# A scheduled attention and feed-forward kernel: the flag branch ahead of a split last output, GpSimd's normalisation as subtract and multiply, and a scheduler that knows the time of queued transposes

## The chip, the cores and the metric

One Trainium2 chip, one of its cores. The metric is the device time of one execution in microseconds (us). In the profile PE is TensorE (matmul), PEld its weight loads, DVE is VectorE, ACT ScalarE, POOL GpSimd and SP SyncE. The granted clock is the share of TensorE's full clock that the profile records; "half clock" is a stretch at 0.5. An execution more than 1.5% above the fastest of its kernel is called slow; only fast ones are compared, and of a kernel that ran once the state is unknown.

## The reference

A pre-norm transformer block: 2048 rows of 512, 32 heads of 16, a hidden width of 1792, no learned norm weights.

```python
h  = x + A(layernorm(x))          # A: qkv = x @ wqkv; softmax(q k^T / 4) v; @ wo
h2 = h + B(layernorm(h))          # B: (gelu(x @ w_gate) * (x @ w_up)) @ w_down
```

## The kernel before

Every piece of work is an `Op` with an engine and a duration. When the kernel is built, a greedy list scheduler plays these durations through and fixes the order of instructions on each engine. Streams of work have priorities with a small random addition (`random.Random(9)`), so each seed gives another order. The softmax has 2048 tiles of 128 x 512 scores; ScalarE makes the exponentials of most of them, two tiles at a time, and VectorE the rest with integer tricks, four at a time. A fast path runs first; if a check finds the data out of its range (flag not 128), an exact path runs after it. Four parts matter here.

The normalised rows that K, Q and V are projected from. Rows 0 to 1023 are done on VectorE, rows 1024 to 2047 on GpSimd, and the latter are transposed by a DMA that SyncE issues:

```python
def ln1_norm(c, t):                       # tile t = 128 rows, c = t // 4
    if c < 2:
        yield Op("dve", 0.327, ...tensor_scalar(xn, x, mean, rstd, subtract, mult))
    else:
        yield Op("pool", 0.2,  ...tensor_tensor(htmp, mean, rstd, mult))
        yield Op("pool", 0.25, ...tensor_scalar(htmp, htmp, -1.0, mult))
        yield Op("pool", 0.77, ...tensor_scalar(xn, x, rstd, htmp, mult, add))
    # then: c < 2 TensorE transposes, else dma_start_transpose (SyncE)
```

How the scheduler counts a DMA, whatever its kind:

```python
self.t[op.eng] = start + 0.5
self.pipe = max(start + 1.5, self.pipe) + op.dur / 0.32
self.done[tok] = self.pipe + 0.8
```

The last output tile: 14 matmuls of 512 columns, one VectorE addition of the residual, one DMA. And the end of each engine's program:

```python
P.run(name, h)                            # everything of the fast path
h.wait_ge(P.sems["dve"], P.flag_count)
h.reg_load(r, flag[0:1, 0:1])
with h.If_ne(r, 128):
    ...                                   # the exact path
if name == "sp":
    for k, v in P.dma_count.items(): h.wait_ge(P.sems[k], v)
```

## Time and profile before

| | before |
|---|---|
| time, three executions | 818.12 us (818.0 to 818.47) |
| the profiled execution | span 820.5, granted clock 0.992 (it took 822.24) |
| ScalarE's first exponential / last one ends | 14.38 / 791.03 |
| from there to the end | 29.5 us |
| exponentials on ScalarE, groups on VectorE | 776, 124 |

The table is read as three stretches: up to the first exponential (the head), the run of exponentials (ScalarE's bound: 742.9 us busy of 754.2 from 36.87 to 791.03), and the tail after it. The first part of the run, in which ScalarE still stands idle between groups of eight, is called the ramp. The lines themselves stand in the prediction.

### The profile page before, as it was taken

How to read it: one execution, taken by the hardware profiler on the slowest of the kernel's cores; microseconds unless marked ns; L12 is line 12 of the kernel's file. 1: busy time of each engine (PE TensorE's matmuls, PEld its weight loads, DVE VectorE, ACT ScalarE, POOL GpSimd, SP SyncE). 2: the span in 40 equal slices, each digit the busy share in tenths (PEclk: the TensorE clock that was granted, in tenths of full speed). 3: DMA queues.
4: the chain of work that ended last, by engine and by line, in shares of the span. 5: the costliest groups of instructions: out<-in, count | busy, mean ns of one | idle time of the engine just before them, and what ended most of it. 6: DMA issues, size and time to landing. Idle time of an engine off the chain costs nothing.

```text
span 820.5 us, 20261 instructions
## 1 busy us (share of the span) xinstructions
PE 780.9 (95%) x8247; PEld 278.0 (34%) x8325; DVE 759.1 (93%) x1238; ACT 766.9 (93%) x809; POOL 251.5 (31%) x305
## 2 busy tenths in 40 slices
PE   7999999999999999999989999999999999999997
PEld 3322222222222222222223333333343444444555
DVE  7669999999999999999979999999999999999974
ACT  4799999999999999999989999999999999999961
POOL 5713355423333221221333223223232231342220
PEclk9999999999999999999989999999999999999999
DMA  6200000700110000010021000001010200110000
GB/s 206 52 8 1 7 8 7 276 21 8 26 40 14 14 8 1 14 34 14 8 40 34 20 9 21 20 17 32 8 20 15 40 8 8 28 29 16 16 22 18
DMA packets 49879, 24.33 MB, mean 30 GB/s; under 512 B 39281, under 2 KB 48753, under 8 KB 49777
## 3 DMA queue, kind: packets, MB, share of 16 engines
q1 hardware_dynamic: 49776, 22.95, 10.9%
q8 instruction: 67, 1.10, 0.6%
q14 instruction: 36, 0.29, 0.1%
HBM read 11.80 MB, written 2.10 MB: 17 GB/s over the span
## 4 chain that ended last, share of the span: by engine, by line
DVE 37%; PE 35%; ACT 16%; issue 7%; DMA 3%; POOL 1%; SPq 0%; DVEq 0%; ACTq 0%; POOLq 0%
PE pbank L1329 21%; DVE dXE L1706 16%; ACT PT L1335 13%; PE pbank L1328 13%; DVE dXE L1721 6%; DVE dXE L1719 5%; DVE dXE L1726 5%; DVE GUT L1972 1%; ACT GUT L1985 1%; DMA OAT<-OA 1%; DVE OA L1810 1%; DMA wqkv_sb<-in_A_wqkv_dram 1%; PE pbank L2052 1%; POOL dXE L1723 1%; ACT L1335 1%
## 5 line engine op out<-in xcount | busy, mean ns | idle before, releaser
L1335 ACT ACTIVATE PT<-pbank 128x1024 bf16<-128x1024 f32 x776 | 722.7, 1081 | 19.2 <-PE pbank L1329 16.7
L1329 PE MATMUL pbank<-QT,KT 32*128 32x512 bf16 (+1 forms) x2304 | 347.1, 360 | 17.8 <-ACT PT L1335 8.1
L1706 DVE TENSOR_SCALAR dXE<-pbank 128x512 uint16<-128x512 f32 x496 | 325.8, 683 | 10.9 <-PE pbank L1329 9.7
L1723 POOL TENSOR_TENSOR dXE<-dXE 128x512 f16<-128x512 f16 x124 | 157.4, 1269 | 376.2 <-DVE dXE L1721 376.2
L1329 PEld LDWEIGHTS pbank<-QT,KT 32*128 32x128 bf16 x2304 | 89.3, 91 | 292.2 <-ACT PT L1335 201.2
L1329 PE MATMUL pbank<-PT,VA 128*32 128x256 bf16 (+2 forms) x2708 | 130.7, 294 | 0.1
L1721 DVE TENSOR_TENSOR dXE<-dXE 128x1536 f16<-128x1536 f16 x124 | 124.0, 1000 | 0.9
L1719 DVE TENSOR_SCALAR dXE<-dXE 128x2048 uint16<-128x2048 uint16 x124 | 92.4, 745 | 0.1
L1726 DVE TENSOR_SCALAR dXE<-dXE 128x2048 uint16<-128x2048 uint16 x124 | 88.0, 713 | 4.8 <-POOL dXE L1723 3.5
L1329 PE MATMUL pbank<-dXE,VA 128*32 128x256 f16 (+2 forms) x1752 | 77.0, 291 | 0.7 <-DVE dXE L1726 0.5
L1328 PE MATMUL pbank<-hnT_c,wg_sb 128*128 128x256 bf16 (+2 forms) x392 | 70.0, 291 | 0.0
L1329 PEld LDWEIGHTS pbank<-PT,VA 128*32 128x32 bf16 x2708 | 48.4, 96 | 61.7 <-issue 58.8
L1328 PE MATMUL pbank<-hnT_c,wu_sb 128*128 128x256 bf16 (+2 forms) x392 | 59.3, 289 | 3.6 <-DVE GUT L2000 3.4
L1328 PE MATMUL pbank<-wd_sb,GUT 128*128 128x512 bf16 x202 | 55.3, 382 | 3.2 <-issue 3.0
L2052 PE MATMUL pbank<-ones_bf,zero_bf 128*128 128x512 bf16 x163 | 55.2, 389 | 2.1 <-issue 2.1
L1832 POOL TENSOR_TENSOR Otok<-OAT,LINV 128x128 bf16<-128x128 bf16 (+2 forms) x52 | 28.6, 564 | 82.9 <-DVE LINV L1826 82.7
L1329 PEld LDWEIGHTS pbank<-dXE,VA 128*32 128x32 bf16 x1752 | 31.1, 96 | 30.9 <-issue 18.3
L2000 DVE TENSOR_TENSOR GUT<-pbank,GUT 128x512 bf16<-128x512 f32 (+1 forms) x57 | 36.8, 674 | 2.5 <-ACT GUT L1985 1.5
L1328 PE MATMUL pbank<-xnT,wqkv_sb 128*128 128x512 bf16 (+1 forms) x152 | 38.4, 349 | 0.2 <-DVE dXE L1706 0.2
L1328 PEld LDWEIGHTS pbank<-hnT_c,wu_sb 128*128 128x128 bf16 x392 | 29.5, 98 | 25.2 <-issue 10.7
L1972 DVE CAST GUT<-pbank 128x512 bf16<-128x512 f32 (+1 forms) x53 | 35.6, 674 | 1.0 <-PE pbank L1328 0.7
L1328 PEld LDWEIGHTS pbank<-hnT_c,wg_sb 128*128 128x128 bf16 x392 | 24.8, 97 | 29.0 <-issue 26.5
(80 smaller groups left out, 344.5 us busy)
## 6 DMA issues: line engine op xcount, KB each, us to landing
xres<-in_A_x_dram SPq DMA_DIRECT2D x16, 128.0 KB, 2.2
out_dram<-out_sb SPq DMA_DIRECT2D x16, 128.0 KB, 1.7
wg_sb<-in_B_w_gate_dram SPq DMA_DIRECT2D x1, 1792.0 KB, 7.0
wu_sb<-in_B_w_up_dram SPq DMA_DIRECT2D x1, 1792.0 KB, 11.0
wd_sb<-in_B_w_down_dram SPq DMA_DIRECT2D x1, 1792.0 KB, 14.8
x_sb<-in_A_x_dram SPq DMA_DIRECT2D x3, 512.0 KB, 8.5
wqkv_sb<-in_A_wqkv_dram SPq DMA_DIRECT2D x1, 896.0 KB, 7.7
x_sb<-in_A_x_dram SPq DMA_DIRECT2D x2, 256.0 KB, 3.0
```

The source lines that it names most:

```text
L1328: return lambda e: e.matmul(o, l, r, start=start, stop=stop)
L1329: return lambda e: e.matmul(o, l, r, start=start, stop=stop, tile_position=tile)
L1335: return lambda e: e.activation(out=o, in_=i, func=func, **kw)
L1706: yield Op("dve", 0.603, lambda e: e.tensor_scalar(out=dXE[G["k"] % NX][:, 0, j, :], in0=pbank[:, b, :], scalar1=XMIN + 1024.0 * CENTER, s ...
L1719: yield Op("dve", 0.07 + 0.133 * n, lambda e: e.tensor_scalar(out=W, in0=X, scalar1=0x3ff, scalar2=0xb800, op0=ALU.bitwise_and, op1=ALU.bi ...
L1721: yield Op("dve", 0.066 + 0.267 * nd, lambda e: e.tensor_tensor(out=W[:, 0:nd, :].bitcast(F16), in0=W[:, 0:nd, :].bitcast(F16), in1=X[:, 0 ...
L1723: yield Op("pool", TPOOL, lambda e, j=j: e.tensor_tensor(out=W[:, j, :].bitcast(F16), in0=W[:, j, :].bitcast(F16), in1=X[:, j, :].bitcast( ...
L1726: yield Op("dve", 0.07 + 0.133 * (h1 - h0), lambda e, h0=h0, h1=h1: e.tensor_scalar(out=X[:, h0:h1, :], in0=X[:, h0:h1, :], scalar1=0x7c00 ...
L1832: yield Op("pool" if turned else "dve", 0.15 + 0.55 / len(slots) if turned else 0.06 + 0.28 / len(slots), lambda e, o4=o4, lx=lx, o_ap=o_a ...
L1972: yield Op("dve", 0.07 + 0.001042 * n * CHUNKS[c], lambda e: e.tensor_copy(out=o_ap, in_=i_ap), reads=[("pb", b)], writes=keys, extra=dE)
L2000: yield Op("dve", 0.07 + 0.001042 * n * CHUNKS[c], lambda e: e.tensor_tensor(out=o_ap, in0=u_ap, in1=o_ap, op=ALU.mult), reads=[("pb", b)] ...
L2052: return Op("pe", TMM, lambda e: e.matmul(pbank[:, b, :], zero_bf[:], ones_bf[:], start=False, stop=False, skip_group_check=True), reads=[ ...
```

## The change

The intent, from the code: (a) take SyncE's and ScalarE's flag branch before the last output's instructions, so that its cost lies beside other work, and let ScalarE write the last output in two halves, with the residual added by TensorE through an identity matmul; (b) tell the scheduler how long queued transposes take, and try a new seed; (c) start sooner: ones of V on VectorE, the second 512 rows' norm at a higher priority, two transpose copies on ScalarE; (d) on GpSimd, one instruction subtract-then-multiply in place of three. Cut to its core:

```diff
-        self.rng = random.Random(9)
+        self.rng = random.Random(43)
@@ the scheduler's DMA
+            if op.dma[0] in TURNS:
+                self.t[op.eng] = start + 1.25
+                self.done[tok] += TURNS[op.dma[0]]
+TURNS = dict(OAT=2.0, OT=2.0, hT=2.0, xT=0.6)
-TTAB = 1.3
+TTAB = 1.45
@@ the end of each program
-            P.run(name, h)
+            cut = P.cut.get(name, len(P.eng[name].ops))
+            P.run(name, h, 0, cut)
             h.wait_ge(P.sems["dve"], P.flag_count)
             ...
+            if cut < len(P.eng[name].ops):
+                with h.Else():
+                    P.run(name, h, cut)
@@ ones_v: four GpSimd memsets become one on VectorE
@@ ln1: priorities of the second 512 rows from 9 to -4
-        if t >= 4:
+        if t >= 8:        # epsilon added on GpSimd only for rows from 1024
@@ ln1_norm
-            yield Op("pool", 0.2, ... htmp = mean * rstd)
-            yield Op("pool", 0.25, ... htmp = -htmp)
-            yield Op("pool", 0.77, ... scalar1=rstd, scalar2=htmp, op0=mult, op1=add)
+            yield Op("pool", 0.77, ... scalar1=mean, scalar2=rstd, op0=subtract, op1=mult)
@@ ln1_T
-        if t in (0, 1, 2):
+        if t in (0, 1, 2, 4, 5):      # transpose copies on ScalarE
@@ last_down: identity matmul of h, then 14 matmuls of 256 columns, twice;
@@ last_evac: ScalarE copies each half; its DMA from SyncE, then from ScalarE
(cut: sizes assumed for loads, the bank gate of the V projections, the place of one memset,
 SyncE's last waits sorted, and two more priorities)
```

More of the change, by code (lines that the diff above doesn't have):

```diff
@@ L33, in __init__ @@
         self.dma_count = {}
+        self.dma_last = {}
+        self.cut = {}
         self.n_waits = 0
@@ L100, in dma @@
         self.dma_count[semkey] += 16
+        self.dma_last[semkey] = sum(self.dma_count.values())
         tok = (semkey, self.dma_count[semkey])
@@ L148, in finish, with run @@
         self.wait(eng, [(k, v) for k, v in self.dma_count.items() if v > 0])
-    def run(self, name, h):
+    def run(self, name, h, lo=0, hi=None):
         e = self.eng[name]
-        for (fn, waits, sig, dsem) in e.ops:
+        for (fn, waits, sig, dsem) in e.ops[lo:hi]:
             for (k, v) in waits:
@@ L1192, in emit @@
                 FP.run(name, h)
+            if cut < len(P.eng[name].ops):
+                with h.Else():
+                    P.run(name, h, cut)
             if name == "sp":
-                for k, v in P.dma_count.items():
-                    h.wait_ge(P.sems[k], v)
+                for k in sorted(P.dma_count, key=lambda k: P.dma_last[k]):
+                    h.wait_ge(P.sems[k], P.dma_count[k])
         block.tensor(lambda h: emit("pe", h))
@@ L1343, in xl @@
         def xl(c):
-            return d(x_sb[:, 4 * c:4 * c + 4, :], xv[:, 4 * c:4 * c + 4, :], ("x", c), [("x", c)], 0.5)
+            return d(x_sb[:, 4 * c:4 * c + 4, :], xv[:, 4 * c:4 * c + 4, :], ("x", c), [("x", c)], 0.32)
         yield d(x_sb[:, 0:2, :], xv[:, 0:2, :], ("x", 0, 0), [("x", 0, 0)], 0.25)
@@ L1348, in loads @@
         yield w("wq0", 0, 128, 0.3)
-        yield d(x_sb[:, 4:8, :], xv[:, 4:8, :], ("x", 1), [("x", 1)], 0.9)
-        yield w("wB", 640, 1536, 0.35)
+        yield d(x_sb[:, 4:8, :], xv[:, 4:8, :], ("x", 1), [("x", 1)], 1.05)
+        yield w("wB", 640, 1536, 0.70)
         yield xl(2)
-        yield w("wA", 128, 512, 0.42)
+        yield w("wA", 128, 512, 0.25)
         yield xl(3)
-        yield d(wo_sb[:], A_wo.rearrange("(c p) j -> p c j", p=128), "wo", ["wo"], 0.5)
+        yield d(wo_sb[:], A_wo.rearrange("(c p) j -> p c j", p=128), "wo", ["wo"], 0.3)
     def xkey(c, t):
@@ L1368, in ones_v @@
     def ones_v():
-        for q in range(4):
-            yield Op("pool", 0.6, lambda e, q=q: e.memset(VA[:, 4 * q:4 * q + 4, :, 16:17], 1.0), writes=["VA_ones"], gate=lambda: C["exp"] >= 1, port=True)
-        yield Op("pool", 0.1, lambda e: e.memset(VF[:, NVA:NVA + 15], 0.0), writes=["VA_ones"])
+        yield Op("dve", 0.62, lambda e: e.memset(VA[:, :, :, 16:17], 1.0), writes=["VA_ones"])
+        yield Op("dve", 0.1, lambda e: e.memset(VF[:, NVA:NVA + 15], 0.0), writes=["VA_ones"])
     def masks():
+        yield Op("dve", 0.5, lambda e: e.memset(pbank[:, DENSE[0], :], 0.0), writes=[("pb", DENSE[0])])
         for par in range(2):
@@ L1378, in masks @@
                      reads=[("qm", par)], writes=[("qm", par)])
-        yield Op("dve", 0.5, lambda e: e.memset(pbank[:, DENSE[0], :], 0.0), writes=[("pb", DENSE[0])])
         yield Op("dve", 0.1, lambda e: e.tensor_scalar(out=probe[:, 0:1], in0=ident32[:, 0:1], scalar1=1e6, scalar2=XMIN, op0=ALU.add, op1=ALU.max), reads=["ident32"], writes=["probe"])
@@ L1406, in ln1 @@
                 yield Op("dve", 0.1, lambda e, t=t: e.bn_aggr(out=mv[:, t, :], in_=stats[:, t, :]), reads=[("stats", t)], writes=[("mv", t)])
-                if c == 0:
+                if c < 2:
                     yield Op("dve", 0.1, lambda e, t=t: e.tensor_scalar(out=rstd[:, t:t + 1], in0=mv[:, t, 1:2], scalar1=EPS, scalar2=None, op0=ALU.add), reads=[("mv", t)], writes=[("rstd0", t)])
-                sch.add(ln1_rstd(t), 2 + 7 * c if c else -7.5)
-            sch.add(ln1_norm(c, t), 2 + 7 * c if c else -7.5)
+                sch.add(ln1_rstd(t), (-4 if c == 1 else -7.5 if c == 0 else 2 + 7 * c))
+            sch.add(ln1_norm(c, t), (-4 if c == 1 else -7.5 if c == 0 else 2 + 7 * c))
     def ln1_rstd(t):
         tt_ = slice(t, t + 1)
-        if t >= 4:
+        if t >= 8:
             yield Op("pool", 0.25, lambda e: e.tensor_scalar(out=rstd[:, tt_], in0=mv[:, t, 1:2], scalar1=EPS, scalar2=None, op0=ALU.add),
@@ L1427, in ln1_norm @@
         else:
-            yield Op("pool", 0.2, lambda e: e.tensor_tensor(out=htmp[:, tt_], in0=mv[:, t, 0:1], in1=rstd[:, tt_], op=ALU.mult),
-                     reads=[("mv", t), ("rstd", t)], writes=[("nmr", t)])
-            yield Op("pool", 0.25, lambda e: e.tensor_scalar(out=htmp[:, tt_], in0=htmp[:, tt_], scalar1=-1.0, scalar2=None, op0=ALU.mult),
-                     reads=[("nmr", t)], writes=[("nmr", t)])
             yield Op("pool", 0.77,
-                     lambda e: e.tensor_scalar(out=xn_sb[:, t % 8, :], in0=x_sb[:, t, :], scalar1=rstd[:, tt_], scalar2=htmp[:, tt_], op0=ALU.mult, op1=ALU.add),
-                     reads=[xkey(c, t), ("rstd", t), ("nmr", t)], writes=[("xn", t % 8)], gate=ok)
-        sch.add(ln1_T(c, t), 2 + 7 * c if c else -8)
+                     lambda e: e.tensor_scalar(out=xn_sb[:, t % 8, :], in0=x_sb[:, t, :], scalar1=mv[:, t, 0:1], scalar2=rstd[:, tt_], op0=ALU.subtract, op1=ALU.mult),
+                     reads=[xkey(c, t), ("rstd", t), ("mv", t)], writes=[("xn", t % 8)], gate=ok)
+        sch.add(ln1_T(c, t), (-4 if c == 1 else -8 if c == 0 else 2 + 7 * c))
     def turn(o, i, key, reads, writes, **kw):
@@ L1539, in proj_v @@
             mev.prio = T0 + 2 + 1.8 * t
-            b = yield Acquire(reads=rd)
+            b = yield Acquire(reads=rd, gate=None)
             for hf in range(2):
@@ L1849, in ofin @@
         if u == NU - 1:
-            sch.add(check(), base_dl(c) + 60)
+            sch.add(check(), base_dl(c) + 20)
     def leave(c):
@@ L2003, in up_evac, with last_down, last_evac @@
         C["pieces"] += 1
+    def last_down(c, qt):
+        q0 = g_at[c] + 128 * qt
+        for hf in range(2):
+            cs = slice(256 * hf, 256 * hf + 256)
+            b = yield Acquire(reads=["wd"], gate=lambda: C.get(("gut", c), 0) >= len(packs(c)) - 1)
+            yield Op("pe", 0.11, cols=256, fns=[MM(pbank[:, b, 0:256], ident[:], h_c[c][:, qt, cs], True, False)], reads=["ident", ("h", c, qt)], writes=[("pb", b)])
+            yield Wait(lambda: C.get(("gut", c), 0) == len(packs(c)))
+            for f0 in range(0, NFC, 7):
+                fcs = range(f0, f0 + 7)
+                yield Op("pe", 7 * 0.11, cols=256 * 7, fns=[MM(pbank[:, b, 0:256], GUT[:, fc, q0:q0 + 128], wd_sb[:, fc, cs], False, fc == NFC - 1) for fc in fcs],
+                         reads=["wd"] + [("GUT", fc, q0 // 128) for fc in fcs], writes=[("pb", b)])
+            sch.add(last_evac(c, qt, hf, cs, b), -20)
+        C["down"] += 1
+        C[("down", c)] = C.get(("down", c), 0) + 1
+        C["pieces"] += 1
+    def last_evac(c, qt, hf, cs, b):
+        t = first_t[c] + qt
+        oi = t % 2
+        yield Wait(lambda: hasattr(P, "flag_count"))
+        yield Op("act", 0.28, lambda e: e.activation(out=out_sb[:, oi, cs], in_=pbank[:, b, 0:256], func=ACT.Copy), reads=[("pb", b)], writes=[("osb", oi) if hf == 0 else ("osb2", oi)])
+        sch.release(b)
+        yield Op("act" if hf else "sp", 0.06, lambda e: e.dma_start(out=outv[:, t, cs], in_=out_sb[:, oi, cs]), reads=[("osb", oi) if hf == 0 else ("osb2", oi)], writes=[("outd", t, hf)], dma=("outl", hf))
     def downs(c):
         for qt in range(CHUNKS[c] // 128):
+            if c == NC - 1 and qt == CHUNKS[c] // 128 - 1:
+                yield from last_down(c, qt)
+                return
             b = yield Acquire(reads=["wd"], gate=lambda: C.get(("gut", c), 0) == len(packs(c)))
@@ L2043, in check @@
         P.flag_count = P.eng["dve"].count
+        P.cut = {n: len(P.eng[n].ops) for n in ("sp", "act")}
         sch.release(b)
@@ L2082, in fast_path @@
                 continue
-            items.append(("k", j, c, (tu(0) + TUNIT / 4 * c - 3) if j == 0 else tu(2 * j) - 14 + c))
+            items.append(("k", j, c, (-5 if c == 1 else tu(0) + TUNIT / 4 * c - 3) if j == 0 else tu(2 * j) - 14 + c))
         if j:
@@ L2094, in fast_path @@
     sch.add(masks(), 5)
-    sch.add(ones_v(), 5)
+    sch.add(ones_v(), -9)
     for c in range(NCH):
-        sch.add(ln1(c), 2 + 7 * c if c else -7)
+        sch.add(ln1(c), (-3.5 if c == 1 else -7 if c == 0 else 2 + 7 * c))
     sch.add(first(), -7)
```

## The prediction

> **What bounds the kernel now.** I read the page's busy times first, then ScalarE's timeline for where its run of exponentials starts and breaks, then four windows cut at those points, then ScalarE's waits, then VectorE's timeline of the end. The three compute engines all look full on the page, and the chain of work that ended last jumps between them, so neither tells much. The busy times and the costliest group:
>
> ```profile
> PE 780.9 (95%) x8247; PEld 278.0 (34%) x8325; DVE 759.1 (93%) x1238; ACT 766.9 (93%) x809; POOL 251.5 (31%) x305
> ...
> L1335 ACT ACTIVATE PT<-pbank 128x1024 bf16<-128x1024 f32 x776 | 722.7, 1081 | 19.2 <-PE pbank L1329 16.7
> ```
>
> One exponential of two score tiles costs 722.7/776 = 0.931 us of ScalarE (the 1081 ns of one overlap the next). 1552 of the 2048 tiles go this way; the other 496 are made by VectorE in 124 groups of four. ScalarE's start:
>
> ```profile
> 13.18 0.47 ACT L1491 ACTIVATE QT<-pbank,qmask 128x256 bf16<-128x256 f32 x1 [2.83 <-PE pbank L1328]
> 14.38 1.02 ACT L1335 ACTIVATE PT<-pbank 128x1024 bf16<-128x1024 f32 x1 [0.73 <-PE pbank L1329]
> 16.97 6.52 ACT L1335 ACTIVATE PT<-pbank 128x1024 bf16<-128x1024 f32 x7 [1.56 <-PE pbank L1329]
> 29.06 7.44 ACT L1335 ACTIVATE PT<-pbank 128x1024 bf16<-128x1024 f32 x8 [5.57 <-PE pbank L1329]
> 36.87 7.55 ACT L1335 ACTIVATE PT<-pbank 128x1024 bf16<-128x1024 f32 x8 [0.37 <-PE pbank L1329]
> ```
>
> The first exponential starts at 14.38; ScalarE idles 1.56 before the second and 5.57 before the ninth. After eight steps the first 512 keys are used up, and the next projection of K arrives late. The windows (head, ramp, middle, tail):
>
> ```profile
> core 0: us, PE busy (x) PEld busy (x) DVE busy (x) ACT busy (x) POOL busy (x), PEclk, DMA share, GB/s
> 0.00:14.38 14.38, 11.61 (x83) 6.19 (x85) 9.81 (x33) 3.91 (x6) 5.82 (x19) 1.00 0.83 279
> 14.38:36.87 22.49, 20.17 (x116) 6.77 (x117) 16.52 (x39) 14.98 (x17) 18.78 (x48) 0.92 0.20 49
> 36.87:791.03 754.16, 725.80 (x7747) 247.89 (x7821) 718.36 (x1137) 742.90 (x780) 226.13 (x237) 1.00 0.10 25
> 791.03:820.50 29.47, 23.34 (x320) 17.09 (x308) 14.43 (x31) 5.14 (x7) 0.79 (x2) 0.95 0.07 22
> ```
>
> In the middle ScalarE is busy 742.9 of 754.2 us, so ScalarE bounds it, with 11.3 us of idle left; VectorE has 36 idle there. Its waits in that window are all for TensorE:
>
> ```profile
> ACT PT L1335 <- PE pbank L1329: 8.9, 24, 1.5
> ```
>
> About 3.2 of those 8.9 fall into one spot, 416 to 422 us, where the granted clock is 0.50:
>
> ```profile
> 414.90:421.70 6.80, 6.43 (x45) 1.71 (x46) 4.71 (x8) 3.81 (x5) 2.76 (x2) 0.50 0.26 61
> ```
>
> The tail, 29.47 us, is a latency chain up to the last normalised tile and then TensorE back to back. Its last lines on VectorE:
>
> ```profile
> 801.39 0.42 DVE L1871 COPY hnT_c<-pbank 128x512 bf16<-128x512 bf16 x1 [0.79 <-PE pbank L1911]
> ...
> 807.00 0.13 DVE L2042 CAST flag<-pbank 1x1 int32<-1x1 f32 x1
> ...
> 814.67 0.69 DVE L2021 TENSOR_TENSOR out_sb<-pbank,h_c 128x512 bf16<-128x512 f32 x1 [2.45 <-PE pbank L1328]
> ```
>
> No compute follows 815.37, yet the span ends at 820.50. The trace's records of uncounted instructions fill those 5.1 us on SyncE: output DMA issued 815.39 (0.33), load of the flag 815.78 (0.53), compare-and-branch 816.35 (0.06), then nothing until 819.04 while two 8 KB instruction fetches run (816.78, 817.31), then 17 semaphore waits 0.06 apart to 820.05, then the closing barrier to 820.50. The output itself landed 3.0 after issue, near 818.4: the branch, not the transfer, sets the end.
>
> [...]816.41 to 819.04 is 2.63 us; ScalarE's own branch at 807.67 reaches its next instruction at 810.19, 2.5 us.
> [...]392 ns for the 128x256 Gelu.
> [...]The trace shows half clock at 22.4 to 25.8 and 414.9 to 421.7, though why there no view shows.
> [...]1.7 median issue to landing for the outputs.
>
> **The change part by part.**
> (1) *Split between engines.* The order listing of the built kernel has 782 exponentials for 776 and 121 VectorE groups for 124. ScalarE gains 6 x 0.931 = **+5.6 us**. VectorE loses 3 groups, each four 0.657 conversions, 0.745, 1.000 and 0.710, so 5.1, in all 15 us; but VectorE had 36 idle and does not bound.
> (2) *Head and ramp.* The ones of V (four POOL memsets, 14.21 to 16.96, just when POOL is wanted for the LN of tiles 5 to 7: the mean and variance of tile 5 wait from 15.0 to 17.1) become one VectorE memset[...], in VectorE's idle 0 to 2.6. The LN of the second 512 rows is put forward, two transpose copies move to ScalarE, and V projections no longer stand in front of the fourth tile's transpose on TensorE (1.0 us wait for weights plus 0.4 at 11.2). By hand with the durations above: fourth xn at 10.7, its transposes 11.1, copy 12.25, projections 12.75, Q 13.3, first scores 13.4, first exponential 13.8 instead of 14.4. Scores and V now alternate, so the second need not wait 1.56. VectorE's list from there (each operation at its row's time) puts the last copy of the second 512 rows at 21.8, K at 22.8, its copy at 24.2, the ninth exponential at 24.7. ScalarE, with its two copies (1.2) among the eight, is done at 22.5. I allow 0.4 for a half-clock window: 25.1 against 29.06, **-4.0 us**.
> (3) *Transposes timed as read.* SyncE needs 1.19 per transpose issue (records), and landing is 2.4 median but 10.7 at worst; the scheduler had assumed 0.5 to issue. Now it issues instructions later behind them. This can only remove waits. Of the 11.3 idle I choose to keep 8.5: half of the half-clock spot (1.6) and about 1.2 of the small waits go: **-2.8 us**.
> (4) *Tail up to the last matmul.* After the last exponential TensorE has 42 down-equivalents of 0.216 where it had 50, 32 value products where it had 96, 18 gate matmuls of the next-to-last chunk where it had 24. Following the chain (OA copy, transposes, reciprocal, Otok, OnT, projection, add, statistics, norm, transposes, copy) I get the last normalised tile 9.5 after the last exponential where it was 11.0. From there TensorE has the same gate, up and down work (12.7 before) plus two identity matmuls. But the flag's branch now stands on ScalarE between the first and the second gate's Gelu: the flag comes behind the other chunk's last down, about 16.05 after the last exponential; plus 0.1, 0.5, 0.05 and 2.5 gives 19.15 for the second Gelu. Gelus 1.5, products on VectorE, last product at 21.5; the two halves of the down (14 matmuls of 0.11 each) end at 24.0. Before, TensorE ended 814.64 - 791.03 = 23.6 after it. So +0.4: the branch's cost is partly moved, not removed.
> (5) *After the last matmul.* Before: 820.50 - 814.64 = 5.86. After: half copy 0.4, DMA about 2.0, wait and barrier 0.5, so 2.9: -3.0. The 17 waits fall into the flight. VectorE's own branch (last product 21.5 plus 3.9 as before) ends at 25.4, TensorE's at 24.0 + 1.9 = 25.9, the output at 26.9: the output leads by 1.0. (4) and (5) together **-2.6 us**.
> Sum: 5.6 - 4.0 - 2.8 - 2.6 = -3.8; 818.1 - 3.8 = **814.3 us**.
>
> **Rivals.**
> A: *ScalarE's bound takes it back.* If the idle stays at 11.3, the six exponentials eat most of head and tail: 817. For it: the middle is 98.5% busy. Against: VectorE, 15 us lighter, frees banks and buffers earlier.
> B: *The ScalarE branch becomes the wait.* If its stall is longer than 2.5, or Gelu and products line up worse, the tail gains nothing: 817. For it: TensorE runs out of work about 0.8 before the second product. Against: the up and gate matmuls (4 us) lie beside the stall.
> C: *Waits in the middle were the scheduler's misjudged transposes.* Then idle falls to 4 or so: 810. Against: only 2.4 us of VectorE's waits name a transpose.
> D: *The half-clock windows move.* One more costs about 3, one less gains 3.
>
> **Range and chances.** A and B together give 818 to 819, C with a lost half-clock window 808 to 809; errors of 2 in head and tail each are likely. Range 809.0 to 818.2. Over 2% faster would need 16 us, more than the whole middle idle and all of the end: 3%. Over 2% slower: 1%. Within 2%: 96%.
>
> **What would show it right or wrong.** Right: 782 exponentials near 728 us busy; ninth at about 25; last exponential about 790; on ScalarE a gap near 3 us between the first and second Gelu from the last chunk's gates; end of span about 3 after the last matmul, with no instruction fetch between. Wrong: idle in the middle of 11 or more (then A), a tail of 29 (then B), middle idle under 6 (then C), or half clock at other places (then D). If the ninth exponential is still near 29, step (2) failed.

Passages that no run of this case shows are cut out of it. No term of the sum is among them: it still comes to 5.6 - 4.0 - 2.8 - 2.6 = -3.8, so 814.3 us. Some of its durations are estimates. The 0.11 for a matmul of 256 columns is half of the 0.216 read for 512 (the changed kernel's start 0.109 apart); the 0.4 for the half copy rests on the 392 ns of the 128x256 Gelu (measured 383 ns); the "about 2.0" for its DMA lies near the median of 2.1 of the four outputs in the tail before (64 KB then took 3.3 from SyncE and 1.9 from ScalarE); and the 0.4 allowed for half clock before the ninth exponential is an allowance without working (the profile before has 3.41 us of half clock there, 22.39 to 25.80).

## The result

| | before | after |
|---|---|---|
| time, median (4 executions each, same rounds) | 818.3 us (818.0 to 818.77) | 821.91 us (821.82 to 822.01) |
| ratio | | 1.0044, 95% interval 1.0026 to 1.0061 |

Ratios here are the mean time of one kernel's fast runs over the mean of the other's in the same rounds, so they are not quite the ratio of the medians quoted. The change made the kernel 0.44% slower. 814.3 had been predicted, and 821.9 lies above the range. Within 2%, as the chances said, but the sign is wrong.

The changed kernel's busy times and costliest group:

```profile
PE 782.7 (95%) x8241; PEld 275.8 (34%) x8321; DVE 745.7 (91%) x1220; ACT 771.5 (94%) x819; POOL 249.1 (30%) x277
...
L1347 ACT ACTIVATE PT<-pbank 128x1024 bf16<-128x1024 f32 x782 | 725.7, 1099 | 19.1 <-PE pbank L1341 17.2
```

The 782 exponentials are there, and so is the lighter VectorE. What is new is found where ScalarE's run starts. ScalarE's timeline of the changed kernel (start, duration, instruction, count, and in brackets the idle before it and what ended it):

```profile
23.27 7.45 ACT L1347 ACTIVATE PT<-pbank 128x1024 bf16<-128x1024 f32 x8 [1.39 <-PE pbank L1341]
38.01 6.63 ACT L1347 ACTIVATE PT<-pbank 128x1024 bf16<-128x1024 f32 x7 [7.29 <-PE pbank L1341]
47.14 1.02 ACT L1347 ACTIVATE PT<-pbank 128x1024 bf16<-128x1024 f32 x1 [2.50 <-PE pbank L1341]
49.71 1.94 ACT L1347 ACTIVATE PT<-pbank 128x1024 bf16<-128x1024 f32 x2 [1.54 <-PE pbank L1341]
52.35 8.36 ACT L1347 ACTIVATE PT<-pbank 128x1024 bf16<-128x1024 f32 x9 [0.70 <-PE pbank L1341]
```

The ninth exponential starts at 23.27, nearly 6 us sooner than before and sooner than predicted. Then ScalarE stands idle for 7.29 us before the seventeenth, and again three times: 12.0 us in four gaps. TensorE's timeline shows what it waited for in the middle of the first gap:

```profile
34.10 1.87 PE L1340 MATMUL pbank<-xnT,wqkv_sb 128*128 128x512 bf16 x4 [4.18 <-DMA xnT<-xn_sb]
```

It waited 4.18 us for the DMA that transposes normalised rows, and then it ran at half clock: these four matmuls take 1.87 us, where a group of four takes 1.03 at full clock (at 21.03 in this profile). The granted clock was half at 34.1 to 37.5 and again at 47.7 to 51.1. So the transposes came late, and their input comes from GpSimd. The groups of instructions, changed kernel first, kernel before second:

```profile
L1440 POOL TENSOR_SCALAR xn_sb<-x_sb,mv,rstd 128x512 bf16<-128x512 bf16 x8 | 16.7, 2086 | 1.0 <-issue 0.3
```

```profile
L1433 POOL TENSOR_SCALAR xn_sb<-x_sb,rstd,htmp 128x512 bf16<-128x512 bf16 x8 | 6.1, 767 | 1.0 <-issue 0.3
...
L1430 POOL TENSOR_SCALAR htmp<-htmp 128x1 f32<-128x1 f32 x8 | 1.8, 224 | 0.7
L1428 POOL TENSOR_TENSOR htmp<-mv,rstd 128x1 f32<-128x1 f32 x8 | 1.5, 190 | 0.2
```

The one instruction that replaced three takes 2086 ns. The three together took 767 + 224 + 190 = 1181 ns. Each of the eight tiles therefore costs GpSimd 0.9 us more, instead of 0.4 less. The GpSimd timeline repeats every 3.05 us (2.09 for this, 0.57 and 0.23 for the reciprocal root, and gaps), and the last of its eight transposes is issued at 43.83 where it was at 37.68.

ScalarE's timeline of the tail:

```profile
804.48 0.60 ACT L1975 ACTIVATE GUT<-pbank 128x512 bf16<-128x512 f32 x1 [3.65 <-PE pbank L1340]
812.47 1.36 ACT L1975 ACTIVATE GUT<-pbank 128x512 bf16<-128x512 f32 x3 [7.39 <-PE pbank L1340]
815.82 0.38 ACT L2032 ACTIVATE out_sb<-pbank 128x256 bf16<-128x256 f32 x1 [1.99 <-PE pbank L1340]
817.46 0.38 ACT L2032 ACTIVATE out_sb<-pbank 128x256 bf16<-128x256 f32 x1 [1.25 <-PE pbank L1340]
```

Between the first and the second Gelu lie 7.4 us. The idle is named after TensorE, but only its first part is TensorE's: the last gate matmuls that the second Gelu needs stand in a group that runs from 808.72 to 809.67. The records of uncounted instructions show ScalarE loading the flag at 809.51, branching at 810.00 and going on at 812.47, so the last 3.0 us are the flag and the branch. After the last half copy comes the DMA (issued 817.87), SyncE's last wait passes at 819.79, and the span ends at 820.27, about 2.8 us after the last matmul. SyncE's own branch, at 810.02, was over when it issued the next output at 812.70.

### The profile page after: what moved, and what is told of

Read it like the earlier page. It is cut to its first block, busy times and chain, and to the rows that moved or that the text cites. A ratio compares the mean times of both kernels' runs of the same rounds, so it can differ in the third digit from the quotient of the medians.

```text
span 820.3 us, 20211 instructions
## 1 busy us (share of the span) xinstructions
PE 782.7 (95%) x8241; PEld 275.8 (34%) x8321; DVE 745.7 (91%) x1220; ACT 771.5 (94%) x819; POOL 249.1 (30%) x277
## 4 chain that ended last, share of the span: by engine, by line
PE 46%; ACT 24%; DVE 15%; issue 9%; POOL 1%; DMA 1%; ACTq 0%; DVEq 0%
PE pbank L1341 29%; ACT PT L1347 23%; PE pbank L1340 15%; DVE dXE L1713 7%; PE pbank L2087 2%; DVE dXE L1728 2%; DVE dXE L1726 2%; DVE dXE L1733 1%; ACT GUT L1992 1%; POOL dXE L1730 1%; DVE GUT L1979 1%; DMA xnT<-xn_sb 1%; POOL xn_sb L1440 1%; ACT L1347 0%; DVE OA L1817 0%
## 5 line engine op out<-in xcount | busy, mean ns | idle before, releaser
L1347 ACT ACTIVATE PT<-pbank 128x1024 bf16<-128x1024 f32 x782 | 725.7, 1099 | 19.1 <-PE pbank L1341 17.2
L1341 PE MATMUL pbank<-QT,KT 32*128 32x512 bf16 (+1 forms) x2304 | 344.8, 360 | 13.4 <-ACT PT L1347 5.1
L1713 DVE TENSOR_SCALAR dXE<-pbank 128x512 uint16<-128x512 f32 x484 | 318.9, 680 | 12.0 <-PE pbank L1341 10.1
L1730 POOL TENSOR_TENSOR dXE<-dXE 128x512 f16<-128x512 f16 x121 | 152.8, 1263 | 373.6 <-DVE dXE L1728 373.6
L1728 DVE TENSOR_TENSOR dXE<-dXE 128x1536 f16<-128x1536 f16 x121 | 119.6, 989 | 1.1
L1733 DVE TENSOR_SCALAR dXE<-dXE 128x2048 uint16<-128x2048 uint16 x121 | 85.2, 708 | 7.5 <-POOL dXE L1730 5.0
L1726 DVE TENSOR_SCALAR dXE<-dXE 128x2048 uint16<-128x2048 uint16 x121 | 89.4, 739 | 0.2
L1340 PE MATMUL pbank<-wd_sb,GUT 128*128 128x512 bf16 (+1 forms) x219 | 56.5, 368 | 3.7 <-issue 2.7
L2087 PE MATMUL pbank<-ones_bf,zero_bf 128*128 128x512 bf16 x161 | 53.0, 385 | 2.5 <-issue 2.5
L1839 POOL TENSOR_TENSOR Otok<-OAT,LINV 128x128 bf16<-128x128 bf16 (+2 forms) x52 | 25.8, 513 | 77.0 <-DVE LINV L1833 74.6
L1341 PEld LDWEIGHTS pbank<-dXE,VA 128*32 128x32 bf16 x1696 | 29.7, 96 | 30.3 <-issue 18.8
L1531 POOL TENSOR_SCALAR QT<-QT,qmask 128x512 bf16<-128x512 bf16 x30 | 26.2, 880 | 32.8 <-DVE QT L1528 32.0
```

The costliest lines, as they stand in the source:

```text
L1340: return lambda e: e.matmul(o, l, r, start=start, stop=stop)
L1341: return lambda e: e.matmul(o, l, r, start=start, stop=stop, tile_position=tile)
L1347: return lambda e: e.activation(out=o, in_=i, func=func, **kw)
L1531: yield Op("pool", 0.85, lambda e, par=par: e.tensor_scalar(out=QT[:, c, 2 * j + par, :], in0=raw, scalar1=qmask[:, par:par + 1], scalar2= ...
L1713: yield Op("dve", 0.603, lambda e: e.tensor_scalar(out=dXE[G["k"] % NX][:, 0, j, :], in0=pbank[:, b, :], scalar1=XMIN + 1024.0 * CENTER, s ...
L1726: yield Op("dve", 0.07 + 0.133 * n, lambda e: e.tensor_scalar(out=W, in0=X, scalar1=0x3ff, scalar2=0xb800, op0=ALU.bitwise_and, op1=ALU.bi ...
```

## The experiments

Fifteen kernels were run; each ran on one chip, beside the kernel before. All gave correct results unless it is said that they did not.

### The kernel before, once more

No edit. 

> The kernel before, unchanged, for a second profile and the clock of each timed run. Theory (the first profile of before caught a stray half-clock stretch at 414.9 to 421.7, worth about 3.2 us of ScalarE idle, so that its 820.5 us span stands for a slow execution of about 822.2 us while the timed ones took 818.3): most executions take 818.0 to 818.8 with a span near 816.5 and a mean granted clock near 0.996, and have no half clock near 415 us. Rival (the difference between span and time varies from run to run for other reasons): spans of 820.5 with times of 818, or the half clock at 415 in every profile.

Measured: 818.84 us (817.7 to 820.37, 6 executions), ratio 1.0004 (0.999 to 1.0018). Its profile has a span of 816.9. Its ScalarE timeline:

```profile
29.29 7.44 ACT L1335 ACTIVATE PT<-pbank 128x1024 bf16<-128x1024 f32 x8 [6.13 <-PE pbank L1329]
37.10 7.55 ACT L1335 ACTIVATE PT<-pbank 128x1024 bf16<-128x1024 f32 x8 [0.38 <-PE pbank L1329]
45.07 15.15 ACT L1335 ACTIVATE PT<-pbank 128x1024 bf16<-128x1024 f32 x16 [0.42 <-PE pbank L1329]
```

The half clock near 415 us, which the prediction took for a part of the kernel, is not there: ScalarE's 60 and 43 exponentials from 359.52 to 455.61 are broken by one wait of 0.45 us, at 415.69, where the first profile has ScalarE busy for 3.81 of the 6.80 us. So this profile, not the first, is the partner of all that follows. Here one also sees what the ninth exponential's gain was worth: before, once past the ninth (at 29.29), the seventeenth and the twenty-fifth follow almost without idle, the seventeenth at 37.10. After, the ninth is 6.0 us sooner, and the seventeenth 0.9 later.

### Is it the subtraction, the order, or the single instruction?

Three edits of the changed kernel, in GpSimd's instruction alone. They have the same two scalars and the same order of instructions on every engine. All three are **wrong** (relative errors of 0.11 to 0.24), because with the mean and the reciprocal deviation as the two scalars only subtract-then-multiply is right. That wrong values do not move the time is seen in the second: 821.74 us, like the changed kernel's 821.91.

```diff
-  scalar1=mean, scalar2=rstd, op0=ALU.subtract, op1=ALU.mult
+  scalar1=rstd, scalar2=mean, op0=ALU.mult, op1=ALU.add        # norm_mul_add
+  scalar1=rstd, scalar2=mean, op0=ALU.mult, op1=ALU.subtract   # norm_mul_sub
+  scalar1=mean, scalar2=rstd, op0=ALU.add, op1=ALU.mult        # norm_add_mul
```

Multiply, then add: 

> The changed kernel with one edit: the LN normalisation of tiles 8 to 15 on GpSimd multiplies by rstd and adds the mean, where it subtracted the mean and multiplied (slightly wrong on purpose; all other instructions and their order are the same). Theory (the subtract-then-multiply form takes GpSimd 2.09 us where multiply-then-add took 0.77, and this starves TensorE of the third and fourth 512 rows): the op falls to 0.77, ScalarE's idle before the 17th exponential falls from 7.3 to under 1 and all its idle in 23 to 53 us from 12.0 to under 2, the half clock at 34 and 48 us goes, time 810 to 813. Rival (the DMA transposes or the order of SyncE's queue hold K up, not GpSimd): the op falls but the idle stays above 5 and the time above 817. Rival 2 (the ScalarE bound takes it back): idle goes but reappears later, 816 or more.

Multiply, then subtract: 

> As norm_mul_add, but multiply by rstd and then subtract the mean (slightly wrong on purpose). It tells what makes GpSimd slow. If it is the subtraction: about 2.09 us for each of the eight, and the time near 822. If it is the order (anything before the multiply): 0.77 us and 810 to 813.

Add, then multiply: 

> As norm_mul_add, but add the mean and then multiply by rstd (slightly wrong on purpose). If the subtraction is what is slow: 0.77 us and a time of 810 to 813. If it is the order, or anything but one multiply-then-add form: about 2.09 us and near 822.

Measured, in the order of the three: 811.66 us (811.48 to 811.97, 5 executions; ratio to before 0.9913, 0.99 to 0.9926), 821.74 and 811.62 (one execution each, so of unknown state). GpSimd's group in the three profiles:

```profile
L1440 POOL TENSOR_SCALAR xn_sb<-x_sb,rstd,mv 128x512 bf16<-128x512 bf16 x8 | 6.2, 771 | 1.0 <-issue 0.3
```

```profile
L1440 POOL TENSOR_SCALAR xn_sb<-x_sb,rstd,mv 128x512 bf16<-128x512 bf16 x8 | 16.7, 2089 | 1.0 <-issue 0.3
```

```profile
L1440 POOL TENSOR_SCALAR xn_sb<-x_sb,mv,rstd 128x512 bf16<-128x512 bf16 x8 | 6.2, 771 | 1.0 <-issue 0.3
```

ScalarE's seventeenth exponential in the first of them (1.28 of idle before it, where the theory had expected under 1):

```profile
31.84 7.55 ACT L1347 ACTIVATE PT<-pbank 128x1024 bf16<-128x1024 f32 x8 [1.28 <-PE pbank L1341]
```

What follows: the subtraction is slow on GpSimd, in either place; the addition in the same places is not. And that one operator is worth 10.3 us of the whole (821.9 against 811.6; 10.1 between the second and the third, in the same rounds). It is all idle of ScalarE: 18.8 us between its first and last exponential in the changed kernel, 8.6 with multiply-then-add. With it gone, the changed kernel is 0.9% faster than the kernel before. No other part of the change has to be blamed for the slowdown.

### A correct mend on GpSimd

The mean is negated by one more small GpSimd instruction, and the large one adds it.

```diff
-  yield Op("pool", 0.25, ... rstd = var + EPS)
+  yield Op("pool", 0.25, [... htmp = mean * -1.0, ... rstd = var + EPS])
-  scalar1=mean, scalar2=rstd, op0=ALU.subtract, op1=ALU.mult
+  scalar1=htmp, scalar2=rstd, op0=ALU.add, op1=ALU.mult
```

> The changed kernel with its LN of tiles 8 to 15 mended and right: GpSimd negates the mean in one more small instruction beside the one that adds epsilon, and then adds and multiplies (0.77 us) where it subtracted and multiplied (2.09). The order of instructions on TensorE, ScalarE, VectorE and SyncE is that of the changed kernel. Theory (the subtraction on GpSimd is the whole reason that the change did not pay): correct, 811.3 to 812.3, like the two wrong ones with an add, no half clock, idle of ScalarE before the 17th exponential near 1.3. Rival (the negation's 0.22 us per tile on the same engine costs K again): over 813.

Measured: 815.72 us (815.26 to 817.49, 6 executions), ratio 0.9963 (0.9944 to 0.9981). The rival was right. Its ScalarE timeline has more idle in the ramp than multiply-then-add had (there 1.28 before the seventeenth and 0.42 before the twenty-fifth):

```profile
32.41 6.64 ACT L1347 ACTIVATE PT<-pbank 128x1024 bf16<-128x1024 f32 x7 [1.85 <-PE pbank L1341]
40.42 1.02 ACT L1347 ACTIVATE PT<-pbank 128x1024 bf16<-128x1024 f32 x1 [1.37 <-PE pbank L1341]
43.63 6.63 ACT L1347 ACTIVATE PT<-pbank 128x1024 bf16<-128x1024 f32 x7 [2.18 <-PE pbank L1341]
```

With 0.24 us more per tile on GpSimd (the negation), this profile has a mean granted clock of 0.96 from 13.4 to 53.0, which is about 3 us of half clock, where multiply-then-add had 1.00; and the time is 4 us longer. The half clock does not come every time: the profile of the late branch below has the same GpSimd chain and a like wait of ScalarE (1.30 us before the exponential at 40.95, here 1.37 before that at 40.42), and a mean clock of 1.00 over the whole span.

### The subtraction alone, put into the kernel before

```diff
-  three GpSimd instructions (product, negation, multiply and add)
+  yield Op("pool", 0.77, ... scalar1=mean, scalar2=rstd, op0=subtract, op1=mult)
```

> The kernel before with only the LN of tiles 8 to 15 in the form of the change: one subtract-and-multiply on GpSimd in place of a product, a negation and a multiply-and-add; the scheduler believes 0.77 us for it. Theory (that form takes 2.09 us, so each tile costs GpSimd about 0.9 more than the three it replaces, and the third and fourth K come some 3 and 7 us later): slower than before by 4 to 9 us, 822 to 828, with idle of ScalarE before the 17th exponential of 3 or more. Rival (K was late in the changed kernel only because it had reached that point earlier): within 2 us of before.

Measured: 852.65 us (851.12 to 853.98, 4 executions), ratio 1.0412 (1.0385 to 1.0439): far worse than any theory said. Its profile has half clock throughout 32.0 to 79.0 (clock 0.50; 1.00 from 79.5 to 126.5), and ScalarE meanwhile gets its exponentials one at a time:

```profile
36.73 1.02 ACT L1335 ACTIVATE PT<-pbank 128x1024 bf16<-128x1024 f32 x1 [0.48 <-PE pbank L1329]
38.24 1.02 ACT L1335 ACTIVATE PT<-pbank 128x1024 bf16<-128x1024 f32 x1 [0.49 <-PE pbank L1329]
```

Here one exponential every 1.51 us (28 in the 47.0 us) where the kernel before has a mean of 0.93: during the half clock TensorE is the bound, counted busy for 45.15 of the 47.0 us, ScalarE for 28.43. This run is no pure one, since fewer declared instructions also gave the scheduler another order (782 exponentials). So it neither prices the subtraction nor shows that the subtraction set off the half clock; the new order, without the slow instruction, was not run.

### The tail alone, on the kernel before

All of part (a), nothing else. The scheduler then puts ScalarE's branch behind all of its Gelus.

```diff
+ cut, Else branch, sorted waits, last_down, last_evac, flag check 40 priority units earlier
```

> The kernel before with only the tail of the change: flag loaded and branch taken ahead of the last output, last output in two halves of 256 columns by ScalarE, waits sorted. 776 exponentials as before; here the scheduler places ScalarE's branch after all of its Gelus. Theory (the branch's instruction fetch, 2.6 us, and the 17 waits, 1.0, leave the end): 814.5 to 815.7 against 818.7, the span ending about 2.8 to 3.3 after the last matmul where it was 5.9. Rival (the branch on ScalarE or a slower DMA from ScalarE's queue takes its place): over 817.

Measured: 816.79 us (815.45 to 818.7, 6 executions), ratio 0.9973 (0.9953 to 0.9993). From the last exponential's end (788.38) to the end of the span:

```profile
788.38:815.10 26.72, 23.86 (x339) 18.64 (x325) 13.59 (x30) 5.91 (x9) 0.79 (x2) 1.00 0.08 24
```

26.7 where the kernel before has 816.9 - 787.5 = 29.4: the tail part gains 2.7 us by itself. The time shows about 2, between what the theory and the rival had expected; the mean granted clock of its six executions was 0.996 to 0.998.

### ScalarE's branch after the last Gelu

The mend with the extra GpSimd instruction, with the cut moved.

```diff
-  yield Wait(lambda: hasattr(P, "flag_count"))
+  yield Wait(lambda: hasattr(P, "flag_count") and C.get(("gelu", c, len(packs(c)) - 1), 0))
+  P.cut.setdefault("act", len(P.eng["act"].ops))
```

> As fix, but ScalarE takes its flag branch after the Gelus of the last chunk and ahead of the two output copies, not between the first and the second Gelu. Theory (the branch stalls ScalarE 2.5 us while TensorE runs out of work, some 1.5 us of the tail): the Gelus follow the gate matmuls at once, and the last matmul ends 0.5 to 1.5 us sooner, 810.3 to 811.3. Rival (then the branch delays the first output copy as much as it had delayed the Gelus): 811.5 to 812.5, the same as fix.

Measured: 815.25 us (813.77 to 816.84, 6 executions), ratio 0.9957 (0.9938 to 0.9976). The tail in the profile is 25.7 us where it was 26.3, but executions of both kernels overlap. See the same edit below.

### The second eight norms on VectorE

The correct mend that leaves GpSimd only the reciprocal root. The schedule keeps the order of the changed kernel on ScalarE and SyncE, and moves two rows on TensorE.

```diff
 def ln1_norm(c, t):
-    if c < 2:
+    if c < 4:
         yield Op("dve", 0.327, ... op0=ALU.subtract, op1=ALU.mult)
```

> A correct mend: the changed kernel, but the eight layer-norm products of rows 1024 to 2047 (subtract, then multiply) run on VectorE instead of GpSimd, where the same form took 2.09 us; the first eight already run on VectorE at about 0.39 us. The order of instructions on ScalarE and SyncE stays exactly that of the changed kernel, on TensorE two rows move. Theory (the late third and fourth K come from the slow GpSimd subtraction and from nothing else): 17th exponential near 32 instead of 38.0, ramp idle about 2 to 3 instead of 12, no half clock in the ramp, 811.0 to 812.8, as the numerically wrong multiply-then-add variant (811.66). Rival (VectorE, which gets 8 x 0.39 = 3.1 us more in the ramp, now delays the copies of K and V): ramp idle 5 or more and 814 to 816, no better than the mend with one more GpSimd instruction (815.72).

Measured: 812.29 us (812.03 to 812.51, 6 executions), ratio 0.9916 (0.9898 to 0.9933). The theory was right. VectorE does the same subtract-then-multiply in 0.395 us, and has the room (busy for 21.41 of the 26.70 us from 13.30 to 40.00). ScalarE's timeline:

```profile
23.13 7.44 ACT L1347 ACTIVATE PT<-pbank 128x1024 bf16<-128x1024 f32 x8 [1.41 <-PE pbank L1341]
32.46 7.55 ACT L1347 ACTIVATE PT<-pbank 128x1024 bf16<-128x1024 f32 x8 [1.89 <-PE pbank L1341]
40.43 20.48 ACT L1347 ACTIVATE PT<-pbank 128x1024 bf16<-128x1024 f32 x22 [0.42 <-PE pbank L1341]
```

The seventeenth exponential is at 32.46 where it was at 38.01, and in all six executions the mean granted clock was 1.00. **This version is correct and beats both kernels**: 0.84% below the kernel before by the ratio, and some 9.6 us below the changed one (medians of different rounds).

### The same, with ScalarE's late branch

> As norms_dve, and ScalarE's flag branch stands after the last chunk's last Gelu, ahead of the two output half copies, instead of between the first and second Gelu. Theory (the 2.4 us stall between the Gelus lies on the path to the last product): from last exponential to the end 25.7 instead of 26.4, so 0.7 less than norms_dve: 810.3 to 812.1. Rival (the branch only moves onto the path of the half copies): same as norms_dve within 0.2.

The edit is that of the late branch above. Measured: 813.56 us (811.71 to 819.11, 6 executions), ratio 0.994 (0.9912 to 0.9969). The profiled execution had a span of 809.9 against 810.3, a gain of 0.4; the others scatter up to 819 with clocks down to 0.99. No gain is shown. Moving the branch takes the stall out from between the Gelus (the idle before the second falls from 7.44 us to 4.41), but it then stands in front of the first half copy (2.90 us idle before it where it was 1.99). Why its executions scatter more is open.

### Transposes timed as read: three seeds, with and without

The prediction gave this part 2.8 us. It can be built without it, but then the scheduler's whole order changes, so one pair cannot tell the part from the luck of the draw. Hence three pairs, all on the correct mend with the norms on VectorE.

```diff
-            if op.dma[0] in TURNS:
-                self.t[op.eng] = start + 1.25
-                self.done[tok] += TURNS[op.dma[0]]
```

```diff
-        self.rng = random.Random(43)
+        self.rng = random.Random(9)      # or 1
```

Seed 43 without: 

> As norms_dve, without the part that tells the scheduler the time of queued DMA transposes (it again counts 0.5 us for the issue and nothing more for landing). This prices step 3 of the prediction, which gave that part 2.8 us of middle idle. The built kernel has 779 exponentials on ScalarE instead of 782, 3 x 0.93 = 2.8 us less. If the part is worth 2.8 us: middle idle about 8 instead of about 5 and the same time as norms_dve or up to 1 more after the split gives 2.8 back, 811 to 813.5. Rival (the timing alters nothing that waits): idle stays near 5, and with three exponentials less 808.5 to 810.5.

Seed 9 with: 

> As norms_dve (VectorE norms, transposes timed), with the scheduler's random seed of the kernel before, 9, instead of 43; 780 exponentials instead of 782. Theory T (timing the transposes as read is what took the middle idle from about 9 to 6, and it was worth 11 us of idle with seed 43): 810 to 815, middle idle under 8. Rival S (each order is a draw, and 43 was a lucky one for the timed scheduler; the part by itself is worth little): anything, 812 to 830, middle idle well above 8.

Seed 9 without: 

> As seed9, without the timing of the transposes; 782 exponentials. T: at least 5 us slower than seed9, middle idle at least 5 us larger. S: within a draw of seed9, either way.

Seed 1 with: 

> As norms_dve, with seed 1, which neither kernel used; 780 exponentials. T: 810 to 816, middle idle under 8. S: 812 to 830.

Seed 1 without: 

> As seed1, without the timing of the transposes; 780 exponentials. T: at least 5 us slower than seed1, middle idle at least 5 us larger. S: within a draw of seed1, either way.

In the table, the time is the median of the fast executions, and the idle is ScalarE's from 40 us to its last exponential, worked out from the windows (length less busy) of the one profiled execution.

| seed | timed: us | timed: idle | not timed: us | not timed: idle |
|---|---|---|---|---|
| 43 | 812.29 (812.03 to 812.51) | 5.9 | 833.61 (824.92 to 834.14) | 17.3 |
| 9 | 822.12 (819.68 to 828.94) | 7.5 | 829.07 (828.69 to 829.6) | 15.9 |
| 1 | 816.84 (816.36 to 817.12) | 7.5 | 826.74 (825.79 to 826.79) | 13.9 |

The windows that the first row comes from, with the timing and without:

```profile
40.00:784.03 744.03, 735.04 (x7797) 245.13 (x7796) 704.41 (x1114) 738.13 (x779) 219.36 (x233) 1.00 0.10 25
```

```profile
40.00:801.50 761.50, 746.79 (x7783) 248.22 (x7783) 705.08 (x1106) 744.21 (x780) 221.08 (x232) 0.99 0.10 24
```

The ratios to the kernel before are 0.9916 against 1.0126, 1.0048 against 1.0115 and 0.9965 against 1.0083; a fourth execution of seed 43 without the timing, 838.72, was slow and is left out. All three pairs of medians have the same sign: with the timing there is 6 to 11 us less idle and 7 to 21 us less time. For seed 9 alone the sign is not clear of noise (one timed execution took 828.94 at a clock of 0.987, and the intervals of the ratios, 0.9974 to 1.0122 and 1.0096 to 1.0135, overlap). For seed 43 part of the distance is half clock, at least 17.0 us of it in the profile without the timing (clock 0.50 from 203.2 to 220.2); its one execution at a clock of 1.00 took 824.92, still 12.6 above the timed median. The seed matters as well: with the timing the three stand 10 us apart, and seed 9 missed the 810 to 815 of theory T. Much of that lies in the tail, which is 26.3, 32.2 and 22.3 us long for seeds 43, 9 and 1. So both theories are right in part, and in these three pairs the part is worth more than predicted. But the old kernel has no such timing and only 747.49 - 739.56 = 7.9 us of idle there (the repeated profile). Either the rest of the change would add a wait that the timing keeps away, or the old kernel's order, of which only seed 9 was run, was a lucky draw; no run here tells these two apart, nor which of the other edits (priorities, the table-load time, the new head) would add the wait. One expectation was wrong in a plain number: the version of seed 43 without the timing has 784 exponentials, not the 779 written down, a miscount.

## Why the prediction was wrong

The ledger uses the repeated profile of the kernel before (span 816.9), the changed kernel's (820.3) and the mend's with norms on VectorE (810.3). "Busy" and "idle" are ScalarE's between its first and last exponential, from the windows.

| us | predicted | after | mend |
|---|---|---|---|
| first exponential starts | -0.6 | -0.1 | -0.3 |
| ScalarE busy (exponentials, two copies) | +6.8 (5.6 and 1.2) | +4.1 | +4.0 |
| ScalarE idle | -7.4 (-4.6 and -2.8) | +2.5 | -7.2 |
| tail | -2.6 | -3.1 | -3.1 |
| span | -3.8 | +3.4 | -6.6 |

The predicted -4.0 up to the ninth exponential is split here into its parts: -0.6 for the start, +1.2 for the copies, hence -4.6 of idle. The windows behind the measured columns (length, then busy time of PE, PEld, DVE, ACT and POOL, then clock), kernel before (repeated), then changed kernel, then the start of the mend (its rest stands above):

```profile
13.56:40.00 26.44, 24.35 (x136) 7.85 (x135) 17.66 (x40) 17.98 (x20) 19.55 (x49) 0.87 0.23 56
40.00:787.49 747.49, 733.43 (x7799) 246.57 (x7801) 717.22 (x1135) 739.56 (x778) 225.79 (x236) 1.00 0.10 25
```

```profile
13.46:40.00 26.54, 20.95 (x126) 6.37 (x129) 17.05 (x42) 17.85 (x21) 20.77 (x24) 0.94 0.19 48
40.00:53.00 13.00, 10.02 (x53) 2.29 (x52) 3.47 (x5) 8.26 (x9) 3.62 (x4) 0.87 0.10 21
53.00:793.96 740.96, 718.49 (x7703) 244.28 (x7774) 702.92 (x1112) 735.54 (x776) 219.26 (x233) 1.00 0.10 25
```

```profile
13.30:40.00 26.70, 25.59 (x161) 7.50 (x160) 21.41 (x53) 23.39 (x26) 8.13 (x19) 1.00 0.25 66
```

Length less the ACT figure is the idle: before 8.5 + 7.9 = 16.4, after 8.7 + 4.7 + 5.4 = 18.8, mend 3.3 + 5.9 = 9.2. The loss lies ahead of 53 us, and behind it there is a gain. The idle of the mend fell by 7.2 us, where 7.4 had been predicted: the prediction describes a kernel without the slow subtraction.

**Step (2), head and ramp: this step failed.** It ended its account at "the ninth exponential" and booked that as -4.0 for the whole kernel. The ninth did come, at 23.27, even 1.8 us sooner than the predicted 25.1. But a gain there lasts only if the next K follows, and nothing in the step asked when the third and fourth K come. They hang on GpSimd's norms. The prediction's step never priced the new form of that instruction, although the diff changes it; it silently let the declared 0.77 stand. Measured: 2.09. Nor could the step's own sign of failure, a ninth exponential still near 29, show this, since it looks no further than the step did. The timing experiments show this cause: with the addition in its place, 811.6; with the subtraction, 821.7 to 821.9.

**The half clock on top.** Idle of TensorE turned into slower TensorE. In the changed kernel TensorE waits 4.18 us, until 34.10, and has half clock from 34.08 to 37.49; it waits 2.82 us, until 46.17, and has half clock from 47.73 to 51.14. From 12 us on these are its only waits of more than 1.2 us. The first profile of the kernel before does not show the same: it has half clock at 22.39 to 25.80 with no wait over 0.6 us in the 3.41 us before, and at 414.92 to 421.74 after a wait of 1.31 us; its waits of 1.35 us (until 307.03) and 1.33 us (until 503.25) were followed by none. In the 3.41 us before these four stretches TensorE was counted busy for 0.00, 1.56, 2.22 and 1.87 us. So both long waits here came with half clock; what exactly sets it off is not shown. Rival D named moving half-clock windows, but as chance; here both come with the waits for the late transposes, and with the addition in place of the subtraction both are gone (clock 1.00 from 13.3 to 53 us).

**Step (1), the split: right in kind, too large.** 5.6 was predicted for six exponentials. Busy time rose by 725.7 - 722.3 = 3.4 us between the changed kernel and the repeated profile of the kernel before, so each costs less than the mean of 0.931 that was used: the mean itself fell to 725.7/782 = 0.928 us. That fewer of them follow an idle, after which one takes 1.02 where the next in a row add 0.92, would explain part of it (they form 65 unbroken groups where the first profile of the kernel before has 82); no run tests that.

**Step (3), transposes timed as read: near in size, its reason not shown.** Behind the ramp (from 53 us) the idle of the changed kernel is 5.4 us, under the 6 that was to speak for rival C. But the step's base of 11.3 held the stray half clock, and the step booked half of it, 1.6, as a gain on the 818.1 us of executions that did not have it. The repeated profile has 7.9 - 0.4 = 7.5 from there, so the saving is about 2, near the 2.8. SyncE needs 1.20 us to issue a transpose in the changed kernel (median of 69), where the scheduler of the kernel before counted 0.5. That the timing made this saving is not shown; what the three seeds show is that without it the new code is 7 to 21 us slower.

**Steps (4) and (5), the tail: right.** Predicted 26.9 from the last exponential to the end, measured 26.3. The second Gelu starts 18.5 after the last exponential (19.15 predicted). The gap before it is 7.4, not the "near 3" that was to be seen: 2.5 of it is ScalarE's branch (810.00 to 812.47), and with the branch moved behind the Gelus 4.4 of the gap remain. The end comes 2.8 after the last matmul where 2.9 was predicted. Run alone, with ScalarE's branch behind the Gelus, the tail part gains 2.7.

**Rivals A and B** together (818 to 819) came nearest in time, but neither has the mechanism: with the subtraction gone, the gain of head and tail stays.

## What to carry to other kernels

When an edit swaps one form of an instruction for another, take the new form's duration from a run and not from the duration declared; here one operator out of two turned 0.77 us into 2.09 and a gain of 0.8% into a loss of 0.4%. Follow a start-up gain through every later link that feeds the same engine, up to the point where it runs without idle, because the first link that stays late takes the gain back. And where a scheduler decides the order, test an edit with more than one seed: here the seed alone was worth 10 us (812.3 against 822.1).
